# An attention chunk and a gated FFN on one core: 384-token blocks in one written order, ones beside v, sums inverted by Ln and Exp, long-row loads

## The chip, the cores and the metric

One core of a Trainium2 chip runs the program. The metric is the device time of one execution in microseconds (us), the median of several executions. Every run is of one core, so a run counts as slow only when it lies over 1.5% above the fastest of the same kernel; every time and ratio below is from fast runs. Each kernel also has one profiled execution. The profile's span (first to last instruction) is 1 to 2 us shorter than the measured time.

Engines: PE multiplies matrices, DVE and POOL are elementwise engines, ACT applies functions, SP only issues transfers. In both kernels POOL also issues the transfers that convert a type on the way. In the traces here each engine works through its instructions in the order in which they were written (POOL's copies of 0.2 us below start at 46.6 us, right behind the casts and issues that stand before them).

## The reference

Four batches of 768 tokens, 8 heads of 64. Attention is local: a chunk of 32 queries sees its own 32 keys, 16 before, 8 after, and 8 memory rows. The result goes through a gated FFN of width 1536.

```python
for c in range(nc):                      # chunks of 32
    k_full = concat(mem_k, k[c*32-16 : c*32+40]);  v_full likewise
    scores = q_c @ k_full.T / sqrt(64)
    a = exp(scores - max);  a = a / sum(a)
    out[c] = a @ v_full
x = out as (tokens 3072, 512)
y = (relu(x @ w_gate) * (x @ w_val)) @ w_out      # float32 out
```

## The kernel before

The kernel takes 96 queries with a band of 120 keys and 8 memory rows as one unit of work. It loads the bands of a whole batch, and starts FFN work for 384 tokens when the attention of those is done. FFN units are slipped between attention units by a queue.

```python
def load_q_dma(b, hp, dma):              # POOL queue: float32 to bf16 on the way
    for hh in range(2):
        dma(qin_bf[:, :, hh, :], q[b, h0 + hh].rearrange("(st p) d -> p st d", p=128))
# k: bands of 120 rows of 256 bytes, overlapping, on the SP queue, cast on DVE
# v: the same bands on the POOL queue, with a transfer for the ones column
...
def stage2():
    for hh in range(2):
        nc.tensor.matmul(sT_ps, lhsT=kT_ext[...], rhs=qT_pair[...], start=True, stop=True)
        nc.scalar.activation(expT[:, hh, :], sT_ps, ACT.Exp, scale=SCALE)
    nc.vector.tensor_tensor(out=expT, in0=expT, in1=mask, op=ALU.mult)
def stage3():                            # queries come out on partitions
    for hh in range(2):
        nc.tensor.matmul(o_ps[:, hh, :], lhsT=expT[:, hh, :], rhs=vres[:, qb, hh, :], ...)
    nc.vector.reciprocal(rinv, o_ps[:, :, D:D + 1])
    nc.vector.tensor_tensor(out=x_big[...], in0=o_ps[:, :, 0:D], in1=rinv_b, op=ALU.mult)
# x_to_xT: four transposes per 96 tokens, then copies
...
for hp in range(HP): res_tiles[hp].qin = load_q_dma(0, hp, pool_dma)   # whole batch
for hp in range(HP): res_tiles[hp].kstg = load_k_dma(0, hp, sp_dma)
for hp in range(HP): res_tiles[hp].vstg = load_v_dma(0, hp, pool_dma)
load_weights()                           # three transfers, on the POOL queue
```

The softmax here doesn't subtract the row's maximum and nothing guards it: scores larger than these inputs give would overflow.

## Time and profile before

| | before |
|---|---|
| time, median (lowest to highest) | 347.97 us (347.11 to 349.10, 4 runs) |
| span of the profiled run | 346.4 us |
| first gate matmul of the FFN | 90.0 us |
| from there to the end | 256.4 us |
| DMA packets | 105,326 |

The page of the profile cuts the span in 40 slices of 8.7 us. A digit is the busy share in tenths.

```profile
span 346.4 us, 5865 instructions
...
PE   0300670014999999999999999999999999999995
...
POOL 9977970028899997411299800000000000000000
PEclk9999999999999999999999999999999999999999
DMA  6999999999999999956369900200010010002002
```

For ten slices PE does little while the DMA row stands at 9; from then on PE is full. The chain of waits, followed back from the last instruction, says the same as shares of the span, by engine and by line:

```profile
PE 73%; DMA 15%; POOL 9%; ACT 1%; issue 1%; DVE 0%; ACTq 0%; POOLq 0%
```

The window view gives busy time per stretch: start and end, length, then each engine's busy us and number of instructions, the granted clock, the DMA share and GB/s.

```profile
core 0: us, PE busy (x) PEld busy (x) DVE busy (x) ACT busy (x) POOL busy (x), PEclk, DMA share, GB/s
0.00:91.00 91.00, 26.00 (x183) 15.94 (x184) 25.39 (x124) 17.87 (x89) 59.20 (x113) 1.00 1.37 147
91.00:121.20 30.20, 30.20 (x215) 16.90 (x213) 20.62 (x90) 14.01 (x51) 30.20 (x42) 1.00 1.12 72
```

PE is busy 26 of the first 91 us, and all of the 30.2 us after. (The DMA column can exceed 1, as its 1.37 and 1.12 here do.)

### The profile page before, as it was taken

The page shows a single profiled execution, that of the slowest core. Times are in us where ns is not written, and L with a number is a line of the kernel's source. Part 1 is how long each engine was busy: PE and PEld are TensorE (multiplying, and loading weights), DVE is VectorE, ACT ScalarE, POOL GpSimd, SP SyncE. Part 2 cuts the span into 40 slices and gives each one's busy share as a digit, 9 for nine tenths or more (in the row PEclk, how much of TensorE's full clock was granted, in tenths as well). Part 3 has the DMA queues.
Part 4 walks back from the last instruction along what each step waited for, and adds up shares of the span by engine and source line. Part 5 has one row for each costly group of instructions (what it writes and reads, how often), then busy time and mean ns, then how long its engine had stood idle before and what let it go on. Part 6 is the DMA issues. An engine that isn't in the chain of part 4 may idle for free.

```text
span 346.4 us, 5865 instructions
## 1 busy us (share of the span) xinstructions
PE 275.6 (80%) x1920; PEld 153.8 (44%) x1920; DVE 169.6 (49%) x752; ACT 129.4 (37%) x473; POOL 138.2 (40%) x220
## 2 busy tenths in 40 slices
PE   0300670014999999999999999999999999999995
PEld 0100440002465555555554565465555545554641
DVE  1102762005477648645882775376547736762420
ACT  1300450002355344645642554455345425432321
POOL 9977970028899997411299800000000000000000
PEclk9999999999999999999999999999999999999999
DMA  6999999999999999956369900200010010002002
GB/s 122 165 141 122 90 137 209 196 170 138 116 64 62 64 176 159 104 82 114 25 34 111 75 2 1 83 10 3 30 62 1 2 61 32 2 2 91 0 15 78
DMA packets 105326, 27.27 MB, mean 79 GB/s; under 512 B 99664, under 2 KB 101200, under 8 KB 105296
## 3 DMA queue, kind: packets, MB, share of 16 engines
q0 software_dynamic: 67376, 12.22, 49.7%
q1 hardware_dynamic: 37920, 14.69, 21.3%
q8 instruction: 15, 0.25, 0.3%
q14 instruction: 15, 0.12, 0.1%
HBM read 32.51 MB, written 6.29 MB: 112 GB/s over the span
## 4 chain that ended last, share of the span: by engine, by line
PE 73%; DMA 15%; POOL 9%; ACT 1%; issue 1%; DVE 0%; ACTq 0%; POOLq 0%
PE g_ps L257 20%; PE vl_ps L263 18%; PE out_ps L277 18%; DMA qin_bf<-in_q_dram 13%; PE sT_ps L209 6%; PE o_ps L225 5%; DMA vres<-oz 2%; POOL qin_bf L121 2%; PE xT_ps L243 2%; PE kT_ps L198 2%; PE qT_ps L128 2%; POOL vres L166 1%; POOL vres L167 1%; POOL vres L138 1%; ACT o_sb L282 1%
## 5 line engine op out<-in xcount | busy, mean ns | idle before, releaser
L257 PE MATMUL g_ps<-xT_big,w_gate_sb 128*128 128x384 f16 x384 | 95.5, 332 | 0.4 <-DVE xT_big L244 0.2
L263 PE MATMUL vl_ps<-xT_big,w_val_sb 128*128 128x384 f16 x384 | 81.4, 328 | 0.0
L215 ACT ACTIVATE expT<-sT_ps 128x96 f16<-128x96 f32 x256 | 53.5, 252 | 62.5 <-PE sT_ps L209 62.2
L269 DVE TENSOR_TENSOR gvT<-vl_ps,g_relu 128x384 f16<-128x384 f32 x96 | 53.3, 555 | 36.4 <-PE kT_ps L198 19.4
L277 PE MATMUL out_ps<-w_out_sb,gvT 128*128 128x512 f16 x288 | 68.3, 379 | 1.9 <-ACT o_sb L282 1.8
L268 ACT ACTIVATE g_relu<-g_ps 128x384 f16<-128x384 f32 x96 | 47.4, 493 | 43.2 <-PE g_ps L257 25.3
L200 DVE COPY kT_ext<-kT_ps 128x128 bf16<-128x128 bf16 x128 | 27.7, 217 | 56.7 <-PE kT_ps L198 56.6
L225 PE MATMUL o_ps<-vres,expT 128*96 128x66 f16 x256 | 34.3, 218 | 21.5 <-DMA vres<-in_v_dram 11.5
L263 PEld LDWEIGHTS <-w_val_sb 128*128 128x128 f16 x384 | 35.6, 99 | 21.1 <-issue 1.3
L230 DVE RECIPROCAL rinv<-o_ps 96x2 f32<-96x2 f32 x128 | 20.7, 161 | 47.6 <-PE o_ps L225 40.6
L225 PEld LDWEIGHTS <-expT 128*96 128x96 f16 x256 | 28.4, 130 | 30.1 <-issue 21.2
L277 PEld LDWEIGHTS <-gvT 128*128 128x128 f16 x288 | 27.3, 98 | 31.3 <-issue 3.1
L198 PE MATMUL kT_ps<-ident_b,kres_bf 128*128 128x128 bf16 x128 | 29.7, 232 | 12.3 <-POOL mask_last L94 7.2
L128 PE MATMUL qT_ps<-ident_b,qin_bf 128*128 128x128 bf16 x96 | 14.9, 244 | 30.2 <-DMA qin_bf<-in_q_dram 30.0
L257 PEld LDWEIGHTS <-w_gate_sb 128*128 128x128 f16 x384 | 32.6, 101 | 12.6 <-issue 1.4
L233 DVE TENSOR_TENSOR x_big<-o_ps,rinv 96x128 f16<-96x128 f32 x128 | 36.3, 284 | 2.1
L282 ACT COPY o_sb<-out_ps 128x512 f32<-128x512 f32 x24 | 14.1, 586 | 60.9 <-PE out_ps L277 44.6
L121 POOL DMA_DIRECT2D qin_bf<-in_q_dram x32 | 27.1, 859 | 22.1 <-PE kT_ps L198 16.1
L129 ACT COPY qT_pair<-qT_ps 128x128 bf16<-128x128 bf16 x96 | 18.4, 285 | 46.6 <-PE qT_ps L128 46.5
L209 PE MATMUL sT_ps<-qT_pair,kT_ext 64*128 64x96 bf16 x256 | 35.6, 221 | 0.0
L138 POOL DMA_DIRECT2D vres<-in_v_dram x32 | 29.1, 909 | 12.9 <-DMA w_out_sb<-in_moe_w_out_dram 9.4
L209 PEld LDWEIGHTS <-kT_ext 64*128 64x128 bf16 x256 | 15.0, 94 | 31.5 <-issue 25.1
(36 smaller groups left out, 210.9 us busy)
## 6 DMA issues: line engine op xcount, KB each, us to landing
out_dram<-o_sb SPq DMA_DIRECT2D x24, 256.0 KB, 2.2
kstg<-in_k_dram SPq DMA_DIRECT2D x32, 180.0 KB, 5.3
qin_bf<-in_q_dram POOLq DMA_DIRECT2D x32, 96.0 KB, 4.6
vres<-in_v_dram POOLq DMA_DIRECT2D x32, 90.0 KB, 4.1
kstg<-in_k_dram SPq DMA_DIRECT2D x64, 30.0 KB, 5.6
w_gate_sb<-in_moe_w_gate_dram POOLq DMA_DIRECT2D x1, 1536.0 KB, 11.9
w_val_sb<-in_moe_w_val_dram POOLq DMA_DIRECT2D x1, 1536.0 KB, 19.3
w_out_sb<-in_moe_w_out_dram POOLq DMA_DIRECT2D x1, 1536.0 KB, 28.5
```

The lines of the kernel that those rows point to most:

```text
L121: dma(qin_bf[:, :, hh, :], q[b, h0 + hh].rearrange("(st p) d -> p st d", p=128))
L138: dma(dst[0:BAND, 1:NQB - 1, c0:c1], mid)
L198: nc.tensor.transpose(kT_ps, kres_bf[:, qb].rearrange("p h d -> p (h d)"), ident_b)
L209: nc.tensor.matmul(sT_ps, lhsT=kT_ext[D * hh:D * hh + D, :], rhs=qT_pair[D * hh:D * hh + D, QB * qb:QB * qb + QB], start=True, stop=True,)
L215: nc.scalar.activation(expT[:, hh, :], sT_ps, ACT.Exp, scale=SCALE)
L225: nc.tensor.matmul(o_ps[:, hh, :], lhsT=expT[:, hh, :], rhs=vres[:, qb, hh, :], start=True, stop=True,)
L233: nc.vector.tensor_tensor(out=x_big[:, D * h0:D * h0 + 2 * D].rearrange("p (h d) -> p h d", h=2), in0=o_ps[:, :, 0:D], in1=rinv_b, op=ALU. ...
L257: nc.tensor.matmul(g_ps, lhsT=w_gate_sb[:, f, 128 * m:128 * m + 128], rhs=xT_big[:, f, :], start=(f == 0), stop=(f == NFC - 1),)
L263: nc.tensor.matmul(vl_ps, lhsT=w_val_sb[:, f, 128 * m:128 * m + 128], rhs=xT_big[:, f, :], start=(f == 0), stop=(f == NFC - 1),)
L268: nc.scalar.activation(g_relu, g_ps, ACT.Relu)
L269: nc.vector.tensor_tensor(out=gvT[:, m, :], in0=vl_ps, in1=g_relu, op=ALU.mult)
L277: nc.tensor.matmul(out_ps, lhsT=gvT[:, m, 128 * t:128 * t + 128], rhs=w_out_sb[:, m, :], start=(m == 0), stop=(m == NDC - 1),)
```

## The change

The intent is one pass over eight blocks of 384 tokens, each with its own loads, so that the FFN of block 0 can start early. Attention of block n+1 is written between the FFN units of block n at fixed places.

- k and q come as rows of 1 KB (four tokens to a row), on the SP queue as float32, and are cast on POOL. The transposes then leave tokens in a permuted order, and copies and products with a step of four elements put it right.
- v is the stationary operand, with 64 columns of ones beside it: x comes out transposed, its sums 64 times beside it. No transposes of x.
- The sums are inverted by Ln and Exp on ACT; the masks are the bias of the exponent.
- Weights come in pieces on the POOL queue.

```diff
+def stage_a(n, hp):
+    X = xps.tile([128, 2, 512], F32, name="x_ps")
+    for i in range(NQ):
+        for hh in range(2):
+            nc.tensor.matmul(X[:, hh, QB*i:QB*i+QB], lhsT=vw[:, hp, i, hh, :],
+                             rhs=ex[:, i, :, hh, :], start=True, stop=True)
+    nc.scalar.activation(ln, X[D:128, :, 0:TB], ACT.Ln, scale=1.0 / 64.0)
+    nc.scalar.activation(rinv, ln, ACT.Exp, scale=-1.0, bias=mln64[0:D, :])
+    for hh in range(2):
+        nc.vector.tensor_tensor(out=nat(xT[D*hh:D*hh+D, hp, :]), in0=perm(X[0:D, hh, 0:TB]),
+                                in1=perm(rinv[:, hh, :]), op=ALU.mult)
+# stage_a_wide, for block 0 only: 16 matmuls of 64 output columns put both heads on
+# 128 partitions; one Ln, one Exp, one product of 384 columns
...
+    loads(1, 2)
+    nc.gpsimd.memset(kwins[1][0], 0.0)
+    nc.gpsimd.memset(kwins[1][1], 0.0)
+    for g in range(1, 6):                          # ten weight pieces
+        load_w(wg, moe_w_gate, 256 * g, 256 * g + 256)
+        load_w(wv, moe_w_val, 256 * g, 256 * g + 256)
+    ...                                            # three memsets of vwins[1]
+    casts(1)                                       # on POOL: k, q of 4 head pairs, then v of 4
+    ...                                            # three pieces of w_out
+    PIECES = {0: [("t", 0)], 2: [("s", 0), ("t", 1)], 4: [("a", 0), ("s", 1), ("t", 2)],
+              6: [("a", 1), ("s", 2), ("t", 3)], 8: [("a", 2), ("s", 3)], 10: [("a", 3)]}
+    for n in range(NB):
+        if n + 2 < NB: loads(n + 2)
+        for u in range(NDC + TB // 128):
+            ffn_unit(n, u) or out_unit(n, u - NDC)
+            for what, hp in PIECES.get(u, ()):     # of block n+1; mem_cols on POOL before "t"
+                ...
+            if u == 11: casts(n + 2)
```

t is transposes and copies of k and q, s is scores and exponents, a is the x step.

## The prediction

> **What bounds it now.** The chain of waits gives PE 73% of the 346.4 us, DMA 15%, POOL 9%. The 40-slice view splits the run in two. Until about 91 us PE is mostly idle while the DMA row stands at 9: the run is bound by small packets (50,574 of the 105,326 fall before 91 us; the q casts land as 128-byte packets of 36 ns mean) and by POOL, which issues them; the chain there is q, v and weight loads (29.3 us in one wait for q behind the weights). From 91 us to the end PE is full (slices 11 to 40), so about 255 us of PE work.
>
> PE floor: four 384-column FFN matmuls take 0.65 us in the chain, twelve 512-column ones 2.59 us. That is 12 x 8 x 0.1625 + 3 x 2.59 = 23.4 us per 384 tokens, 187 us in all; before and after alike.[...] The other 68 us of the dense part are attention.
>
> **What changes.** (1) Start: K and Q come as 1 KB rows, V as 256-byte rows, each block only when needed, on the hardware queue; weights in pieces. Fewer packets: about 56,000 by my count. FFN of block 0 can start once 384 tokens of attention are done, not when most of batch 0 is loaded. (2) Attention is regrouped: per head pair and block 8 transposes, 4 matmuls of 192 columns, 8 of 96, so 640 small matmuls against 864. Estimated from 57 ns per 128-column transpose in the timeline and about 70 ns for a 96-column matmul: 1.25 us per pair, 5 us per block. (3) Masking, reciprocal and the x transposes leave DVE and PE; ACT gets 3 exponents of 256 columns, a Ln and an Exp of 768 columns per pair. ACT's slope from 252 ns (96) and 493 ns (384) is 0.84 ns per column plus 172: 2.8 us per pair, 18.9 us per block with relu and output copies. DVE: about 2.6 us per pair, 17 us per block. POOL casts 12 tiles per block[...].
>
> **Sum.** Attention of block 0 ends at about 24 us (DVE 3.4 us per pair, behind the first loads). PE then waits until about 28 us, because POOL must issue ten weight pieces before it casts block 1. Block 0 ends at 60 us; its weights land during it. Blocks 1 to 6: 23.4 + 5 + about 3.5 us of stalls. Two units with three attention pieces give ACT 3.8 us against PE 3.85 us, in one order: relu sits behind Ln, Exp and exponents, and DVE's gate products behind the wait for the inverted sums; with three PSUM banks I expect 0.8 us lost per such pair of units. So 32 us each, 192. Block 7: 23.4. Tail 4. Total 279 us. Nearly all the gain is the start (91 us to about 24-28); the dense part hardly gets faster per token.
>
> Predicted 279 us, range 264 to 297; faster 0.98, same 0.015, slower 0.005.
>
> **What would show it.** First gate matmul near 24-28 us; a PE gap there released by POOL casts; blocks 32 us apart in output writes; PE idle around the Ln/Exp pieces released by ACT relu or DVE gate products; packets near 56,000.
>
> **What would make it wrong.** Weights late in block 0 (adds up to 15 us); stalls in the written order twice as large (+20), or none (-20); strided DVE copies out of PSUM slower than their column count.

60 + 192 + 23.4 + 4 is 279.4, put down as 279. DVE's 2.6 and 3.4 us per head pair and the 0.8 us lost per pair of units are my estimates; the text does not say from which numbers.

## The result, and the profile after

| | before | after |
|---|---|---|
| time, median | 347.97 us | 303.32 us (302.42 to 304.34, 4 runs) |
| span | 346.4 us | 300.8 us |
| first gate matmul | 90.0 us | 27.7 us |
| from there to the end | 256.4 us | 273.1 us |

The ratio of the times is 0.872 (95% interval 0.869 to 0.875). Here and below a ratio is the mean time of one kernel's fast runs over that of the kernel before in the same rounds, so it is not quite the ratio of the medians. The change is worth 12.8%, and the result is correct. The prediction of 279 us was too low, and 303.3 lies above its range. DMA packets fell from 105,326 to 58,716 (about 56,000 forecast).

The first gate matmul came 62.3 us earlier, as forecast. But the rest took 16.7 us longer. The slices (7.5 us each here) show where PE has holes:

```profile
span 300.8 us, 4844 instructions
...
PE   5443447788978899699978897989978897889994
POOL 7293762630044002700152006300180000000000
PEclk9999996999999999999999999899979999999999
DMA  6999999931690049301970179003940110011002
```

The chain of waits has less PE in it, and ACT, DVE and issue time in its place:

```profile
PE 50%; ACT 14%; issue 10%; DVE 8%; DMA 7%; SPq 6%; POOL 4%; POOLq 0%; DVEq 0%; ACTq 0%
```

The window view by block, cut where the last output matmul of each block ends:

```profile
0.00:27.70 27.70, 12.65 (x138) 9.86 (x139) 16.07 (x33) 9.07 (x19) 17.09 (x41) 1.00 1.00 204
27.70:76.90 49.20, 34.39 (x215) 19.18 (x215) 22.28 (x37) 19.52 (x37) 21.11 (x38) 0.93 0.92 161
76.90:109.10 32.20, 28.36 (x214) 17.06 (x213) 21.14 (x36) 18.86 (x36) 7.52 (x16) 1.00 0.47 110
...
173.50:207.30 33.80, 29.78 (x213) 17.85 (x212) 21.32 (x36) 18.85 (x35) 7.52 (x16) 0.95 0.46 104
...
273.40:300.80 27.40, 23.32 (x132) 12.67 (x130) 6.69 (x12) 8.21 (x16) 0.00 (x0) 0.98 0.10 39
```

Block 0 took 49.2 us, 17.0 more than block 1. Four of the six dense blocks took 32.2 us and two 33.9; those two have a granted clock of 0.95. (The clock column is the mean of the trace's clock records. The first of them starts at 94.9 us in the kernel before and at 40.4 us here; where there is none the view prints 1.00, so that a 1.00 earlier than this says nothing: for 27 to 41 us here it prints 1.00, where four 384-column matmuls took 1.27 us and not 0.65. So mean clocks of different runs, such as 0.976 here and 0.932 in e4, can't be compared as they stand.)

What PE waited for in block 0, from the view of waits (total us, times, longest):

```profile
PE sc_ps L202 <- POOL kwin L169: 5.6, 1, 5.6
PE kq_ps L177 <- POOL k L144: 4.1, 1, 4.1
PE sc_ps L202 <- DVE qbd L194: 2.2, 2, 1.2
PE g_ps L267 <- DVE xT L255: 1.2, 1, 1.2
PE v_ps L271 <- ACT gr L274: 0.8, 1, 0.8
```

Both long waits are for POOL. POOL's own timeline (start, length, what; in brackets its idle time before) shows why it was late:

```profile
24.45 0.74 POOL L138 DMA_DIRECT2D wg<-in_moe_w_gate_dram  x1 [1.25 <-DMA wg<-in_moe_w_gate_dram]
26.55 0.74 POOL L138 DMA_DIRECT2D wv<-in_moe_w_val_dram  x1 [1.36 <-DMA wv<-in_moe_w_val_dram]
29.36 0.74 POOL L138 DMA_DIRECT2D wg<-in_moe_w_gate_dram  x1 [2.07 <-DMA wg<-in_moe_w_gate_dram]
31.45 0.74 POOL L138 DMA_DIRECT2D wv<-in_moe_w_val_dram  x1 [1.36 <-DMA wv<-in_moe_w_val_dram]
32.18 1.82 POOL L403 MEMSET vwin<- 128x2048 f16 x1
...
35.23 0.61 POOL L144 CAST k<-kst 112x512 f16<-112x512 f32 x1
...
42.21 2.28 POOL L155 CAST vwin<-vst 128x512 f16<-128x512 f32 x4 [2.47 <-DMA vst<-in_mem_v_dram]
44.44 2.23 POOL L418 DMA_DIRECT2D wo<-in_moe_w_out_dram  x3
46.64 0.38 POOL L169 COPY kwin<-memT 128x32 f16<-128x32 f16 x2
```

Issuing ten weight pieces took from 18.5 to 32.2 us, because four of them, the seventh to the tenth, waited for earlier pieces to land. Whether the queue or the program's own semaphores set that limit is not shown. The k and q casts of block 1 stand behind them, so its first transposes began at 35.9 us. The small copy of memory columns that the first scores need stands behind the v casts, which wait for v to land, and behind three more weight pieces; so the scores began at 46.9 us.

The groups of instructions that the dense blocks turn on (line, engine, operation, names, shapes, count, then busy us, mean ns, and idle time before):

```profile
L236 DVE TENSOR_TENSOR xT<-x_ps,rinv 64x384 f16<-64x384 f32 x56 | 55.8, 996 | 24.7 <-ACT rinv L233 24.3
L186 DVE COPY kwin<-kq_ps 128x360 f16<-128x360 f16 x32 | 30.8, 961 | 16.5 <-PE kq_ps L179 15.6
L231 ACT ACTIVATE ln<-x_ps 64x768 f32<-64x768 f32 x28 | 22.6, 807 | 18.3 <-PE x_ps L228 18.3
L233 ACT ACTIVATE rinv<-ln,mln 64x768 f32<-64x768 f32 x28 | 26.2, 935 | 0.9
L194 DVE COPY qbd<-kq_ps 64x384 f16<-64x384 f16 x64 | 23.4, 365 | 1.0
```

The products and the window copies, which write with a step of four elements, take about twice what I had put down (0.5 us for 384 columns, 0.45 for 360, in my working). In blocks 1 to 3, PE has four waits of 0.8 to 1.2 us, 3.8 us in all. Those of block 2:

```profile
PE sc_ps L202 <- DVE qbd L194: 1.2, 1, 1.2
PE sc_ps L202 <- POOL vwin L155: 1.0, 1, 1.0
PE v_ps L271 <- ACT gr L274: 0.8, 1, 0.8
PE o_ps L280 <- DVE gv L275: 0.8, 1, 0.8
```

### The profile page after: what moved, and what is told of

It reads as the page before. It is cut to its first block, busy times and chain, and to the rows that moved or that the text cites. A ratio compares the mean times of both kernels' runs of the same rounds, so it can differ in the third digit from the quotient of the medians.

```text
span 300.8 us, 4844 instructions
## 1 busy us (share of the span) xinstructions
PE 243.5 (81%) x1753; PEld 145.6 (48%) x1753; DVE 172.3 (57%) x298; ACT 150.0 (50%) x281; POOL 76.2 (25%) x161
## 2 busy tenths in 40 slices
DMA packets 58716, 33.22 MB, mean 110 GB/s; under 512 B 34628, under 2 KB 55620, under 8 KB 58692
## 4 chain that ended last, share of the span: by engine, by line
PE 50%; ACT 14%; issue 10%; DVE 8%; DMA 7%; SPq 6%; POOL 4%; POOLq 0%; DVEq 0%; ACTq 0%
PE o_ps L280 16%; PE v_ps L271 14%; PE g_ps L267 12%; SPq L128 5%; ACT ln L231 5%; ACT rinv L233 4%; DMA vst<-in_v_dram 4%; ACT ex L208 3%; DMA vst<-in_mem_v_dram 3%; DVE xT L236 2%; PE x_ps L228 2%; PE sc_ps L202 2%; DVE kwin L186 2%; DVE qbd L194 2%; PE kq_ps L177 2%
## 5 line engine op out<-in xcount | busy, mean ns | idle before, releaser
L275 DVE TENSOR_TENSOR gv<-v_ps,gr 128x384 f16<-128x384 f32 x96 | 52.0, 557 | 66.8 <-PE v_ps L271 65.1
L271 PE MATMUL v_ps<-xT,wv 128*128 128x384 f16 x384 | 81.1, 335 | 8.4 <-ACT gr L274 8.1
L267 PE MATMUL g_ps<-xT,wg 128*128 128x384 f16 x384 | 82.2, 338 | 1.2 <-DVE xT L255 1.2
L236 DVE TENSOR_TENSOR xT<-x_ps,rinv 64x384 f16<-64x384 f32 x56 | 55.8, 996 | 24.7 <-ACT rinv L233 24.3
L280 PE MATMUL o_ps<-wo,gv 128*128 128x512 f16 x288 | 64.7, 379 | 5.7 <-DVE gv L275 5.7
L274 ACT ACTIVATE gr<-g_ps 128x384 f16<-128x384 f32 x96 | 46.3, 494 | 46.2 <-PE g_ps L267 30.3
L271 PEld LDWEIGHTS <-wv 128*128 128x128 f16 x384 | 38.5, 100 | 39.2 <-issue 16.5
L208 ACT ACTIVATE ex<-sc_ps,bias 128x256 f16<-128x256 f32 x96 | 38.5, 471 | 25.2 <-PE sc_ps L202 15.1
L267 PEld LDWEIGHTS <-wg 128*128 128x128 f16 x384 | 36.6, 101 | 22.1 <-issue 2.9
L186 DVE COPY kwin<-kq_ps 128x360 f16<-128x360 f16 x32 | 30.8, 961 | 16.5 <-PE kq_ps L179 15.6
L194 DVE COPY qbd<-kq_ps 64x384 f16<-64x384 f16 x64 | 23.4, 365 | 1.0
```

What stands on the lines that cost most here:

```text
L186: nc.vector.tensor_copy(kw[:, i0:i0 + NQ - 1, 0:BAND].rearrange("p i (t j) -> p i j t", j=J), src)
L194: nc.vector.tensor_copy(qb[s, :, :, hh, :].rearrange("p i g (j r) -> p (i g) j r", j=J), qps[s].rearrange("p j (g r) -> p g j r", r=8))
L208: nc.scalar.activation(dst, src, ACT.Exp, scale=SCALE, bias=bias[:, g:g + 1])
L236: nc.vector.tensor_tensor(out=nat(xT[D * hh:D * hh + D, hp, :]), in0=perm(X[0:D, hh, 0:TB]), in1=perm(rinv[:, hh, :]), op=ALU.mult)
L267: nc.tensor.matmul(g_ps, lhsT=wg[:, f, 128 * m:128 * m + 128], rhs=xT[:, f, :], start=(f == 0), stop=(f == NFC - 1))
L271: nc.tensor.matmul(v_ps, lhsT=wv[:, f, 128 * m:128 * m + 128], rhs=xT[:, f, :], start=(f == 0), stop=(f == NFC - 1))
```

## The experiments

Theories for block 0: (A) POOL's written order holds PE up; (B) the DMA engines are full until about 43 us (share 1.35 from 27 to 41 us), so that data come late whatever the order; (C) PE's pace behind a gap (four 384-column matmuls in 1.27 us, against 0.65) costs part of it. For the dense blocks: (D) PE waits on the serial chain from the x matmuls through Ln, Exp, products and copies to the scores; (E) the blocks are bound by PE's own work. The edits of e1 to e8 and e12 are each made to the changed kernel alone.

| run | time, median us | ratio to before | block 0, from first gate matmul | block 1 | later blocks |
|---|---|---|---|---|---|
| after | 303.3 | 0.872 | 49.1 | 32.2 | 32.2, 33.9 |
| e1_mem_first | 293.6 | 0.845 | 41.7 | 32.2 | 32.2 |
| e2_kq_first | 297.0 | 0.854 | 45.9 | 32.2 | 32.2, 33.9 |
| e3_both | 296.6 | 0.853 | 43.4 | 32.2 | 32.2, 33.9 |
| e4_warm | 301.2 | 0.866 | 51.4 | 32.2 | 32.2, 33.8 |
| e5_wide | 277.1 | 0.798 | 46.0 | 29.1 | 29.1 |
| e6_t_first | 311.3 | 0.896 | 51.8 | 33.8 | 33.8 |
| e7_perm_out | 291.6 | 0.839 | 49.1 | 30.9 | 30.9, 32.3 |
| e8_no_ln (wrong result) | 280.8 | 0.808 | 46.8 | 29.6 | 29.6 |
| e9_gate | 288.1 | 0.831 | 36.6 | 35.3 | 32.2, 33.8 |
| e10_best | 271.2 | 0.780 | 32.5 | 36.1 | 29.1 |
| e11_best_perm | 271.3 | 0.781 | 32.9 | 36.5 | 29.1 |
| e12_recip | 424.7 | 1.220 | 67.1 | 49.2 | 49.2 to 51.0 |
| e13_all_mem | 265.0 | 0.764 | 32.5 | 29.7 | 29.1 |
| e14_gate_wv | 265.4 | 0.764 | 34.1 | 29.1 | 29.1 |

Block times are from the one profiled execution of each, the times from four (for e9 from its three fast runs; the fourth, 293.1 us, counts as slow). All results but e8's are correct.

### e1: memory columns first

```diff
     nc.gpsimd.memset(kwins[1][1], 0.0)
+    mem_cols(1, 0, pool_copy)
+    mem_cols(1, 1, pool_copy)
     for g in range(1, 6):                # the ten weight pieces
...
-    mem_cols(n + 1, hp, pool_copy)
+    if n or hp > 1:
+        mem_cols(n + 1, hp, pool_copy)
```

> Against the changed kernel's 303.3 us. The memory columns of k for the first two head pairs of block 1 are written on POOL before its ten weight pieces, not behind block 1's v casts. Theory A (POOL's written order holds PE up in block 0): the 5.6 us wait of the first score matmul, 41.3 to 46.9 us, goes, and with it some matmuls at half clock; 295 to 299 us. Theory B (the DMA engines are full until about 43 us, and block 1's v lands only then, whatever the order): the wait moves to the first x matmul of block 1, which needs the v cast at 43 us; 301 to 304 us.

Measured 293.6 us, 9.7 less. Two copies of 0.2 us, moved on POOL, took the 5.6 us wait away. From PE's timeline:

```profile
38.52 1.49 PE L267 MATMUL g_ps<-xT,wg 128*128 128x384 f16 x4
39.80 1.21 PE L271 MATMUL v_ps<-xT,wv 128*128 128x384 f16 x4
40.84 0.49 PE L202 MATMUL sc_ps<-qbd,kwin 128*128 128x192 f16 x4
```

The scores start at 40.8, not 46.9 us. No wait for v took its place: the v casts, done at 43.9, were just in time for the x matmuls at 44.1. Theory A holds for this wait; B as I had put it falls. In the profiled run block 0 is 7.4 us shorter: the wait of 5.6 us, and 1.8 us of matmuls at half pace behind it (below, e4). The median is 1.4 us below my range. The profiled run, the fastest of the four, has none of the two 33.9 us blocks; how many the others have is not known.

### e2 and e3: k and q casts before the weight pieces

```diff
     nc.gpsimd.memset(kwins[1][1], 0.0)
+    (e3: the two mem_cols of e1)
+    casts_kq(1)
     for g in range(1, 6):                # the ten weight pieces
...
-    casts(1)
+    for hp in range(HP):
+        cast_v(1, hp, pool_copy)
```

> Block 1's eight k and q casts are issued on POOL before the ten weight pieces, not after. Theory A: the first transposes of block 1 start at 25 to 29 us, not at 35.9, the 4.1 us PE gap before them goes; 298 to 301 us (the score matmul still waits behind the v casts). Theory B: weight pieces go out later and land later, gate matmuls of block 0 wait for them instead; 302 to 308 us.

> Both moves together. Theory A: both gaps, together 9.8 us, go, and most of the half-clock time behind them (about 5 us); 289 to 294 us, block 0 ends at 62 to 68 us, not 76.9. Theory B: block 0 still ends after 72 us, with a wait for v or weight loads in place of the old ones; 299 us or more.

e2 measured 297.0 us: the transposes start at 31.3 us, right behind the first FFN unit, and the 4.1 us gap is gone. The later score wait is still there, 5.3 us. That is what A had forecast, a little better than its range.

e3 should have gained from both, and was 3 us slower than e1. In its trace both gaps are gone (transposes at 31.2 us, scores at 34.9), and PE is busy for all of 30 to 40 us. But the last FFN unit ends at 54.9 us, and then the output matmuls wait. The waits of e3's block 0:

```profile
PE o_ps L280 <- DMA wo<-in_moe_w_out_dram: 5.1, 3, 2.4
PE v_ps L271 <- DMA wv<-in_moe_w_val_dram: 1.8, 1, 1.8
```

In e3 SP issues v of block 2 from 34.7 to 54.8 us, beside the output weights. So neither theory alone is right: the order on POOL made PE late, and once PE is no longer late, weights are. Whether block 2's loads, which SP issues, take DMA time from the weights, which POOL issues, is not shown by this; e9 tests it.

### e4: keep PE busy while it waits

```diff
+    def filler(count):
+        fill = fps.tile([128, 512], F32, tag="f", name="fill")
+        for _ in range(count):
+            nc.tensor.matmul(fill[:, 0:TB], lhsT=ident, rhs=xTs[0][:, 0, :], start=True, stop=True)
...     # filler(12) before block 1's first t, filler(26) before its first s
```

> The changed kernel's order, with 12 filler matmuls of 384 columns before block 1's first transposes and 26 before its first scores, into a PSUM tile nobody reads, so that PE is not idle while it waits. Theory C (part of block 0's excess is PE at half clock after its gaps: four matmuls of 384 columns in 1.27 us against 0.65): 3 to 5 us less, 298 to 300 us, while the POOL releases stay at 35.9 and 46.9 us. If the clock plays no part: 303 to 305 us.

Measured 301.2 us, 2 us less. In the profiled execution, the slowest of the four, the first filler did what it should, and the second did not last (it ended at 43.2 us):

```profile
31.55 3.92 PE L425 MATMUL fill<-xT,ident 128*128 128x384 f16 x12
...
36.80 0.81 PE L271 MATMUL v_ps<-xT,wv 128*128 128x384 f16 x4
...
46.53 0.82 PE L202 MATMUL sc_ps<-qbd,kwin 128*128 128x192 f16 x4 [3.30 <-POOL kwin L169]
...
49.11 1.49 PE L271 MATMUL v_ps<-xT,wv 128*128 128x384 f16 x4
```

The FFN units at 36 to 39 us ran at full pace (0.65 us from group to group, against 1.27 in the changed kernel), and nothing was gained: the score matmul was released by POOL at 46.5 us all the same. PE then had been idle for 3.3 us and fell to half pace again. So here the half-clock matmuls before the wait for POOL cost nothing; only those behind the last such wait do. Against the same groups at full pace they cost 1.8 us in the changed kernel (46.9 to 50.7 us) and 2.8 us in this execution (46.5 to 52.6 us), whose block 0 is 2.3 us longer than the changed kernel's. The clock record, which begins at 4.5 us in this trace, has half clock from 7.9 to 35.2 us and from 45.5 to 52.3 us, as the paces do. So A's gaps set C off. What C is worth by itself is not tested: no filler was run that lasts until the release. The 2 us of the median are no larger than the spread of these runs, so I take no more than the mechanism from this run.

### e5: the 128-partition x step everywhere

```diff
-    stage_a(n + 1, hp)
+    stage_a_wide(n + 1, hp)
```

> Every block takes block 0's form of the x step: 16 column-tiled matmuls of 64 output columns, one Ln and one Exp of 384 columns on 128 partitions, one product, in place of 8 matmuls, Ln and Exp of 768 columns on 64 partitions and two products. By the durations in the changed kernel's trace this adds about 0.35 us PE per head pair and takes 0.63 us off ACT and 1.0 us off DVE. Theory D (in a dense block PE waits on the serial chain x matmul, Ln, Exp, products, k and q copies, scores: 5.9 us of ACT and DVE against two units of PE): blocks fall from 32.2 us to 30 to 31, 292 to 298 us. Theory E (blocks are bound by PE's own work): blocks grow by 1.4 us, 310 to 313 us.

Measured 277.1 us: 26 less, from one line. The dense blocks fell from 32.2 to 29.1 us. The window of one:

```profile
102.80:131.90 29.10, 28.83 (x245) 16.96 (x244) 16.95 (x32) 15.87 (x35) 7.52 (x16) 1.00 0.50 122
```

PE is busy 28.8 of 29.1 us; its waits in this block sum to 0.2 us. E falls and D stands. The gain was larger than I expected: I had thought of part of the 3.8 us of waits, and nearly all went; the added matmuls cost PE 0.13 us per head pair (x step to next step 0.47 us against 0.34) and not 0.35, which I had read from block 0 where PE ran at half clock. With no waits there was no half clock in the dense blocks either (1.00 in the window above, and no FFN group at half pace after 50 us).

### e6: another order of the pieces

```diff
-    2: [("s", 0), ("t", 1)], 4: [("a", 0), ("s", 1), ("t", 2)], 6: [("a", 1), ("s", 2), ("t", 3)], 8: [("a", 2), ("s", 3)]
+    2: [("t", 1), ("s", 0)], 4: [("t", 2), ("s", 1), ("a", 0)], 6: [("t", 3), ("s", 2), ("a", 1)], 8: [("s", 3), ("a", 2)]
```

> Only the written order of the pieces within a unit changes: transposes, scores, x instead of x, scores, transposes, so that DVE's k and q copies stand ahead of the products that wait for the inverse. Theory D: the two PE waits of 1.2 and 1.0 us per block for the copies go; 30.5 to 31.5 us a block, 294 to 300 us, though gate products and the Ln stand later. If the order is not what costs: 302 to 305 us.

Measured 311.3 us: 8 us slower, a miss. The waits for the copies went, but PE's waits in one block became these:

```profile
PE v_ps L271 <- ACT gr L274: 3.2, 3, 1.3
PE x_ps L228 <- DVE xT L236: 1.1, 2, 0.7
```

The exponents now stand before Ln on ACT, the inverse comes later, and relu, which frees PE's buffers, stands behind all of it. The order costs what it costs because ACT and DVE are both in the chain: moving one piece forward puts another back. The order of the changed kernel was the better of these two.

### e7: unit-step products

```diff
-    out=nat(xT[D*hh:D*hh+D, hp, :]), in0=perm(X[0:D, hh, 0:TB]), in1=perm(rinv[:, hh, :])
+    out=xT[D*hh:D*hh+D, hp, :], in0=X[0:D, hh, 0:TB], in1=rinv[:, hh, :]      # n < NB - 1
...
-    sp(out[row0:row0 + 128, :], o_sb)
+    for g in range(4):                   # the rows of the output put the tokens in order
+        rows = bass.AP(tensor=out.tensor, offset=out[row0 + 32*g, 0].offset,
+                       ap=[[DM, J], [J * DM, 8], [1, DM]])
+        sp(rows, o_sb[32*g:32*g+32, :])
```

> x keeps its permuted token order through the FFN for all blocks but the last, and the rows of the output transfers put it right, so that the products write unit step and not steps of four elements. Stride theory: the product falls from 1.00 us to about 0.55 us (the gate product of the same shape on 128 partitions takes 0.557), 3.5 us of DVE per block; with theory D 30 to 31 us a block, 293 to 298 us. If not the stride but the 64-partition PSUM read sets its time, it stays at 1.0 us and the total at 303.

Measured 291.6 us, 11.7 less; dense blocks 30.9 us. The group of the product:

```profile
L237 DVE TENSOR_TENSOR xT<-x_ps,rinv 64x384 f16<-64x384 f32 x48 | 26.4, 550 | 26.4 <-ACT rinv L233 26.0
```

0.55 us against 0.996, with the same shape and partitions, so it is not the 64-partition read of PSUM. The step of the output is what I take it to be. The edit also flattens the views of the inputs, which read the same elements in the same order; this was not tested apart, but the copies at L194 write in runs of eight elements, also from PSUM, and take 0.365 us for 384 columns. The whole time of the instruction over its 384 columns is 2.6 ns a column (996 ns) for 2-byte elements 8 bytes apart, and 1.4 ns (550 ns) at unit step.

### e8: no Ln, no Exp

```diff
-    nc.scalar.activation(ln, X[D:128, :, 0:TB], ACT.Ln, scale=1.0 / 64.0)
-    nc.scalar.activation(rinv, ln, ACT.Exp, scale=-1.0, bias=mln64[0:D, :])
+    rinv = rconst                        # wrong on purpose
```

> Wrong result on purpose: Ln and Exp of blocks 1 to 7 are left out, and the products take a constant. Takes 1.75 us per head pair off ACT and off the chain between x matmuls and products. Theory D: nearly all PE waits in units 4 to 11 go, blocks of 29 to 30 us, 281 to 289 us. If DVE's amount of work alone binds (21.2 us of 32.2): blocks stay above 31 us.

Measured 280.8 us; blocks of 29.6 us with DVE as busy as ever (21.0 us in a block). So it is not DVE's amount of work that binds, but the length of the chain: shorten it at ACT (e8), at DVE (e7) or at both (e5), and the blocks shrink. This is D.

### e12: a reciprocal on DVE instead

```diff
-    nc.scalar.activation(ln, ...); nc.scalar.activation(rinv, ln, ACT.Exp, ...)
+    nc.vector.reciprocal(rinv, X[D:128, :, 0:TB])
```

> The changed kernel (303.3 us) with the inversion of the sums put back on DVE: one reciprocal of 64 x 768 in place of Ln and Exp on ACT (1.75 us). No trace here has a wide reciprocal; if it ran at the pace of a unit-step DVE operation on PSUM[...] it would take 0.8 us and the total would fall to about 297[...].

The 0.8 us is an estimate of the order that the trace gives: the copies at L194, with 365 ns for 384 columns, would take 0.73 us for 768.

Measured 424.7 us. This undoes one part of the change: inverting on DVE, as the kernel before did for two columns at a time.

```profile
L231 DVE RECIPROCAL rinv<-x_ps 64x768 f32<-64x768 f32 x28 | 138.9, 4959 | 0.9
```

4.96 us for 768 columns, 6.5 ns each, against 1.75 us for Ln and Exp together. With 64-fold sums beside x, Ln and Exp are the cheaper of the two; in the kernel before, where the sum was one column, the reciprocal took 0.16 us.

### e9: hold back block 2's loads

```diff
 e3, and:
+    first = load_k(n, hps)
+    if n == 2:
+        tc.add_manual_dep(first.ins, last_wo.ins.name, SYNC_DEP, reason="order of loads")
...    # last_wo: the last of the three output-weight transfers
```

> e3_both (296.6 us) with one thing more: the loads of block 2 are held until the last output-weight piece has landed. In e3 both PE gaps in front of block 1's attention are gone, but its output matmuls wait for output weights (block 0 ends at 70.7 us, FFN units at 54.8). Theory B' (the rest of block 0's excess is DMA sharing: block 2's k, q and v take the engines from the weights): block 0 ends at 61 to 65 us; 286 to 291 us in all. Rival (the output weights are late because POOL issues them late, behind the v casts): block 0 still ends after 68 us, 294 to 297 us, or block 1 then waits for its own loads and gives it back.

Measured 288.1 us (287.6 to 290.9); the first block took 36.6 us, not 43.4, and no output matmul waited for weights. POOL issued the three output-weight pieces no earlier (39.0 to 40.5 us, against 37.8 to 40.0 in e3), but they landed 7.8 to 11.4 us after their issue, against 17.5 to 22.0. So in e3 the loads of block 2 did take DMA time from the output weights; late issue, the rival, is out. But block 1 now took 35.3 us: part was given back there.

### e10 and e11: the two causes together

> e9_gate with the 128-partition x step of e5_wide in every block. If the two causes add: block 0 about 33 us from its first gate matmul, then six blocks of 29.1 and one of 23.4; 260 to 268 us. If the faster block needs block 2's loads earlier than the gate allows, block 1 grows by what it waits and the total stays at 268 to 274.

> e10_best with the unit-step products of e7_perm_out. With the wide x step a dense block is already at PE's own pace (29.1 us), so DVE time saved there is worth nothing: within 1 us of e10_best, less about 1 us from the first attention, where four products stand in the chain. If DVE still limits the blocks: 3 us or more less.

e10 (e9 with e5) measured 271.2 us. Block 0 took 32.5 us, dense blocks 29.1 as expected, and block 1 took 36.1. e11 adds e7 and is the same within noise (271.3): with PE as full as this, the DVE time saved was worth nothing. PE's longest wait in e10's block 1:

```profile
PE sc_ps L202 <- POOL kwin L169: 4.2, 1, 4.2
```

That is the wait of block 0 once more: memory columns behind v casts, which wait for the loads, which now start later.

### e13 and e14: memory columns first in every block; a looser gate

```diff
     def casts(n):
         casts_kq(n)
+        mem_cols(n, 0, pool_copy)
+        mem_cols(n, 1, pool_copy)
         for hp in range(HP):
             cast_v(n, hp, pool_copy)
...    # on e10; the later mem_cols of these two head pairs are dropped
```

> e10_best (271.2 us) with the memory columns of every block's first two head pairs written on POOL before that block's v casts, as e1 did for block 1 alone. In e10, block 1 takes 36.1 us, 7 over its fellows, 4.15 us of it a score wait at 65 to 69.5 us for a memory-column copy that stands behind v casts. If POOL's order is the cause there too: that wait goes and the half-clock matmuls behind it; block 1 takes 29 to 32 us, 264 to 267 us in all. If the gated loads are the cause: PE waits for v at the first x matmul instead, 269 to 272 us.

> e13_all_mem with the loads of block 2 held only until the last value-weight piece has landed, not the last output-weight piece, so they start some 5 to 8 us earlier, beside the output weights. If the gate makes block 2's loads late in e10: block 1 at 29.1 us and 263 to 265 us in all. If output weights suffer from the sharing as in e3: block 0 ends 2 us or more after 60.1, and the total is 266 us or more.

e13 measured 265.0 us (264.3 to 265.9), block 1 29.7 us: 6.4 of the 7 us were POOL's order again (the score wait fell from 4.2 to 0.5 us), and the gate as such cost the other 0.6 us. e14, where the loads start beside the output weights, measured 265.4, the same within noise: block 1 came to 29.1, block 0 to 34.1 us. What the looser gate gains in one it loses in the other.

e13 is the best version: 0.764 of the kernel before (0.762 to 0.766), and 0.874 of the changed kernel (265.0 over 303.3, medians from different calls).

## Why the prediction was right or wrong

**Right: what bound the kernel, and the main gain.** It put the first gate matmul near 24 to 28 us, and it was at 27.7 (its sum was made with 24). PE's floor for the FFN held: the last block took 23.4 us to the last output matmul, the tail 4.

**Right in the sum: the dense blocks.** 32 us predicted, 32.2 measured in four of six. PE's own part was 28.4 us predicted and 32.2 - 3.8 = 28.4 measured; ACT 18.9 us predicted and 18.9 measured. The stalls were 3.5 predicted, 3.8 measured, but only half of them released as I had said. I expected relu or the gate products to hold PE up some four times for 0.8 us. Each did so once; the other two waits, 1.2 and 1.0 us, were for DVE's copies (one of them is put down to POOL's v cast, but in block 0 and in e1 the same wait is put down to DVE, and the copies end at that moment). So the sum came out partly by luck. DVE's work was mis-sized: 17 us predicted, 21.2 measured, because the strided product took 0.996 us and the window copy 0.961 us, not 0.5 and 0.45. I had named this risk and not costed it.

**Wrong: "PE then waits until about 28 us, because POOL must issue ten weight pieces before it casts block 1. Block 0 ends at 60 us".** This step failed, by 16.9 us: block 0 ended at 76.9. The first half names the right mechanism and mis-sizes it: the transposes of block 1 began at 35.9 and not 28. Of these 7.9 us, 3.3 have nothing to do with the casts: attention of block 0 ended at 27.7 and not 24, and the first FFN unit, at half pace and with a wait of 1.2 us for the last product, kept PE until 31.3 us (where e2, with the casts first, has the transposes). The other 4.6 us are POOL's order (e2). I had taken 0.8 us for each issue (in my working), but four of the ten waited for earlier pieces to land, 6.0 us in all, and three memsets of 3.0 us came next. The second half overlooked a second instance of the same thing: the first scores need a 0.2 us copy that stands on POOL behind casts that wait for v, and behind three weight pieces. That cost a wait of 5.6 us, and 1.8 us of half clock behind it (e1, whose block 0 is 7.4 us shorter). These terms make 15.3 of the 16.9 us; the last 1.6 I do not assign. With those gaps gone, weights would have been the next limit (e3, e9); in the changed kernel itself they hold up no PE instruction in block 0.

**Missed: PE's clock in the dense blocks.** Two of six took 1.7 us more. In one of them, the window from 188 to 191 us has a granted clock of 0.57, right behind two waits of 0.82 and 1.19 us. The clock records in the changed kernel's trace show a grid: every change of clock lies a whole number of 3.413 us steps after the first record, and a half-clock stretch inside the run lasts one or two steps (at one step, half of it, 1.7 us, is lost). Counting the time without a matmul in each full-clock step of the changed kernel (an estimate, since the ends of matmuls are modelled; the end of the run, where PE has no more work, is left out), the three steps with 2.51, 2.01 and 1.96 us were followed by half clock, and all others, with 1.68 us at most, were not. In block 3 the same waits fell into two neighbouring steps, with 0.82 and 1.18 us, and cost no clock. In the experiments' traces, counted in the same way, the smallest idle time before a drop was 1.83 us, and the largest without one 2.03, so these runs show no sharp limit.

The miss of 24.3 us adds up: 16.9 in block 0, 4.5 in blocks 1 to 6 (196.5 against 192: two of them at the lower clock, and 0.2 each), 2.5 between the span of 300.8 and the median time, for which I had allowed nothing, and 0.4 of rounding in my sum.

## What to carry to other kernels

When a kernel has one written order, look for small instructions behind large waits: a 0.2 us copy on a side engine, placed behind a cast that waits for a transfer, cost PE more than 5 us, and moving it was worth 3% of the run. Where PE waits only about 1 us at a time, find the serial chain through the other engines and shorten it anywhere; putting both heads on 128 partitions took time from two engines at once and was worth 26 us. Add up short gaps, too: here 1.96 and 2.01 us of idle time within one step of 3.41 us, in gaps of at most 1.2 us, were each followed by a step at half clock, which cost another 1.7 us. Cost every strided write at the rate that its step has (here 2.6 ns a column with a step of four elements, 1.4 at unit step), not at its column count, and ask of a transfer queue not only what an issue takes (0.74 to 0.97 us here) but when the next issue has to wait for an earlier transfer to land (here six of ten pieces went out in a row, and the other four waited 1.25 to 2.07 us each).
